# Order of two small loads on ScalarE's queue: bias ahead of w_phi

## The chip, the cores and the metric

The kernel runs on one core of one Trainium2 chip. The metric is the device time of one execution in microseconds; the time of a kernel is the median over its runs.

## The reference

The kernel computes one transformer block with two parallel branches on a layer-normed input: linear attention with a learned softmax feature map (w_phi) and an MLP with the Mish activation and a bias b1. S is 2048 tokens, D is 512, there are 32 heads of 16, and F is 1792. All inputs and the output are bf16.

```python
xn = layernorm(x)                                   # (1, 2048, 512)
q, k, v = split(xn @ wqkv)                          # 32 heads of 16 each
pq, pk = q @ w_phi, k @ w_phi                       # per head, 16 x 16
phi_q = concat(softmax(pq), softmax(-pq))           # 32 features
phi_k = concat(softmax(pk), softmax(-pk))
kv, z = phi_k^T v, sum_s(phi_k)
A = (phi_q kv / (phi_q z + 1e-6)) @ wo
h = xn @ w1 + b1
B = (h * tanh(softplus(h))) @ w2
out = x + A + B
```

## The kernel before

The tokens are worked in 16 tiles of 128 and in four groups of four tiles. Layer norm runs per tile: statistics on VectorE (L164, L166), the root on GpSimd (L170, L171), centring on VectorE (L175). The normed tile is transposed into `xnT`, for the first four tiles with TensorE (`ptr`, L562, copied by L581), later by transposing DMAs (L180). w_phi is not applied to keys and queries as such: it is folded into the key and query weights. For that, `Wbd` (L526, VectorE) spreads the loaded w_phi (`wsrc`) into a block-diagonal matrix, the key weights are transposed (`wT`: one half by TensorE, `ptw` L569, copied by ScalarE at L575; the other half by a transposing DMA, L482), and `pfold` (L150) multiplies the two; L159 writes the folded weights back into `wkp`. The first logits (`pl`, L203) use them; `pv` (L188) projects the values with `wv`. `ph` (L222) is the hidden layer, 56 units of four products, and L233 applies Mish with the bias `b1f`.

The bias comes in as a tile of 14 rows of 128 (`b1b`), is transposed by TensorE (`pb`, L535), and VectorE copies it to `b1f` (L622).

The order of the work on each engine is written out by hand: the string `STEPS` lists the steps, and each engine takes its instructions in that order. The first steps matter here:

```python
TW 0 @0; TW 1 @1; LS 0; LS 1; RS 0; PB @2; KM; AZ 0; TK 0 a; RS 1; DX 2; WB; TP 0 @3; F0 0 @4; AZ 1;
TP 1 @5; TK 1 a; FD 0 a; TC 0 v; F0 1 @0; F0 2 @1; FD 1 a; F0 3 @3; FD 2 a; TC 1 v; LS 2; RS 2; FD 3
```

TW is `ptw`, LS, RS and AZ are statistics, root and centring of one tile, PB is the bias transpose, TK the copy into `wT`, WB is `Wbd`, TP and TC the transposes and their copies, F0 and FD fold and write back, KM a small mask, DX a load of tokens, LP the first logits.

The loads of the prologue stand ahead of these steps, in program order, and each goes to the queue of the engine that issues it. SP's queue has token tiles 0 and 1 (L477), half of the key weights into `wkp` (L481), the transposing load (L482), token tiles 2 and 3 (L488), `wv` (L489), the first half of w1 (L490), the next four token tiles (L491), the second half of w1 (L492), and then L598. ScalarE's queue has two loads and a table load (L494). DMA completion semaphores are reused in turn, so an issue from L490 on waits for an earlier load to be complete. TensorE starts with twelve products of constants (`warm`, L512) ahead of its first step.

Of the kernel before, what the change touches and what calls it, by code (L numbers as in the profile page):

```python
# [62 lines left out]
def kernel(  # L63
# [12 lines left out]
    nc = tc.nc  # L76
# [17 lines left out]
    b1_v = B_b1.rearrange("(f p) -> f p", p=P)  # L94
# [21 lines left out]
    b1b = wts.tile([FT, P], BF16, name="b1b")  # L116
# [359 lines left out]
    for t in range(2):  # L476
# [5 lines left out]
    nc.sync.dma_start_transpose(  # L482
        out=wT_of[0][:, :, 2 * P : 4 * P], in_=A_wqkv[2 * P : 4 * P, D : 2 * D]
    )
    with nc.allow_non_contiguous_dma(reason="tiny w_phi load"):
        nc.scalar.dma_start(wsrc[:], wphi_v)
    nc.scalar.dma_start(b1b[:], b1_v[:, :])
    nc.sync.dma_start(x_sb[:, 2:4, :], x_v[:, 2:4, :])  # L488
    nc.sync.dma_start(wv[:], wqkv_v[:, :, 2 * D : 3 * D])  # L489
    nc.sync.dma_start(w1_sb[:, :, 0 : 7 * P], w1_v[:, :, 0 : 7 * P])  # L490
# [183 lines left out]
```

## Time and profile before

| what | value |
|---|---|
| time, median of 3 runs | 174.84 us (174.81 to 175.28) |
| profiled execution, its own time | 173.67 us |
| span of the profiled execution | 171.9 us |
| TensorE busy | 168.4 us, 98% of the span |
| VectorE busy | 145.1 us, 84% |
| ScalarE busy | 118.5 us, 69% |
| w_phi, from issue to landing | 2.4 us |
| granted TensorE clock | 1.00 |

The span runs from the first to the last instruction of one profiled execution; the time of that execution is 1.8 us longer. In the profile PE is TensorE's products, PEld its weight loads, DVE VectorE, ACT ScalarE, POOL GpSimd, SP SyncE; a "q" behind an engine's name is its sequencer, which issues the DMAs. Starts and lengths are in microseconds from the start of the span. The products are pipelined, so the rows of neighbouring ones overlap; the chain of waits lays them end to end.

### The profile page before, as it was taken

Reading aid. Unit: us, or ns where it says so; the run is one execution under the profiler, and the core shown is the slowest. Engines: PE = TensorE matmul, PEld = TensorE weight load, DVE = VectorE, ACT = ScalarE, POOL = GpSimd, SP = SyncE. Lnnn points to the kernel's source line nnn. Section 1 sums busy time; section 2 is a strip of 40 time slices with the busy share of each in tenths; the row PEclk is TensorE's granted clock in tenths of the full one; section 3 lists DMA queues with packets and bytes.
Section 4 is the critical chain, followed back from the end, with each engine's and each line's share of the span. In section 5 each row is a group of like instructions: output and inputs, shape, how many; then the busy total and the mean of one; then the engine's idle time right before and its main releaser. Section 6 shows DMA issues by size and latency. Waiting matters only on the chain.

```text
span 171.9 us, 2727 instructions
## 1 busy us (share of the span) xinstructions
PE 168.4 (98%) x1047; PEld 83.1 (48%) x1047; DVE 145.1 (84%) x224; ACT 118.5 (69%) x191; POOL 9.5 (6%) x26
## 2 busy tenths in 40 slices
PE   8999999999999999999999999999999999999993
PEld 2744444444454454454444744454545444554452
DVE  2878998999689999989999899898899987884333
ACT  2637899997998999899878968966722546632200
POOL 4332103200000000000000000000000000000000
PEclk9999999999999999999999999999999999999999
DMA  5997180689910000000000444036583737769831
GB/s 139 289 373 244 31 215 0 122 135 262 345 57 0 0 4 0 0 0 4 0 0 0 75 90 83 0 59 130 93 159 114 137 83 150 141 141 215 141 101 61
DMA packets 44185, 18.02 MB, mean 105 GB/s; under 512 B 35980, under 2 KB 44172, under 8 KB 44172
## 3 DMA queue, kind: packets, MB, share of 16 engines
q1 hardware_dynamic: 43472, 17.73, 44.1%
q10 hardware_dynamic: 700, 0.12, 0.4%
q8 instruction: 8, 0.13, 0.3%
q14 instruction: 5, 0.04, 0.1%
HBM read 7.10 MB, written 2.10 MB: 53 GB/s over the span
## 4 chain that ended last, share of the span: by engine, by line
PE 98%; DVE 0%; issue 0%
PE po L456 28%; PE ph L222 28%; PE pl L188 14%; PE pv L188 8%; PE po L463 8%; PE warm L512 3%; PE pnd L411 2%; PE pkv L380 2%; PE pfold L150 1%; PE pl L203 1%; PE pwide L188 1%; PE ptr L562 1%; PE ptw L569 0%; DVE x_sb L470 0%; PE pb L535 0%
## 5 line engine op out<-in xcount | busy, mean ns | idle before, releaser
L456 PE MATMUL po<-w_sb,acts 128*128 128x512 bf16 (+2 forms) x238 | 51.0, 366 | 0.0
L222 PE MATMUL ph<-xnT,w_sb 128*128 128x512 bf16 x224 | 49.8, 379 | 0.0
L233 ACT ACTIVATE acts<-ph,b1f 128x512 bf16<-128x512 f32 x56 | 36.3, 698 | 5.4 <-PE ph L222 5.3
L299 DVE TENSOR_REDUCE s<-e 128x128 f32<-128x2048 bf16 x16 | 36.0, 2278 | 1.7 <-ACT e L282 1.7
L222 PEld LDWEIGHTS <-w_sb 128*128 128x128 bf16 x224 | 21.7, 98 | 25.7
L456 PEld LDWEIGHTS <-acts 128*128 128x128 bf16 x238 | 22.2, 98 | 24.2
L282 ACT ACTIVATE e<-e 128x2048 bf16<-128x2048 bf16 x16 | 30.2, 1911 | 0.1
L188 PEld LDWEIGHTS <-xnT 128*128 128x128 bf16 x184 | 17.5, 98 | 20.3 <-DMA wv<-in_A_wqkv_dram 0.5
L470 DVE TENSOR_TENSOR x_sb<-po,x_sb 128x512 bf16<-128x512 f32 (+2 forms) x17 | 11.1, 656 | 8.6 <-PE po L463 8.6
L426 ACT COPY ds<-pnd 128x32 f32<-128x32 f32 x16 | 3.0, 186 | 22.0 <-PE pnd L411 22.0
L188 PE MATMUL pv<-wv,xnT 128*128 128x512 bf16 x64 | 15.8, 379 | 0.0
L246 ACT CAST p_sb<-pl 128x512 bf16<-128x512 f32 x23 | 12.9, 592 | 4.0 <-PE pl L188 4.0
L463 PE MATMUL po<-wqk,xnT 128*128 128x512 bf16 (+2 forms) x68 | 15.4, 366 | 0.0
L188 PE MATMUL pl<-wqk,xnT 128*128 128x512 bf16 x64 | 15.1, 379 | 0.0
L164 DVE BATCH_NORM_STATS2 stats<-x_sb 128x6 f32<-128x512 bf16 x16 | 10.1, 679 | 4.2 <-DMA x_sb<-in_A_x_dram 4.2
L257 DVE TENSOR_TENSOR m<-m 128x512 bf16<-128x512 bf16 (+1 forms) x32 | 11.5, 359 | 1.1
L188 PE MATMUL pl<-wkp,xnT 128*128 128x512 bf16 x48 | 11.8, 379 | 0.0
L257 DVE TENSOR_TENSOR m<-p_sb 128x1024 bf16<-128x1024 bf16 x16 | 10.9, 683 | 0.1
L266 DVE TENSOR_TENSOR e<-p_sb,m 128x2048 bf16<-128x2048 bf16 x8 | 9.8, 1225 | 0.8 <-PE pkv L380 0.5
L266 DVE TENSOR_TENSOR e<-m,p_sb 128x2048 bf16<-128x2048 bf16 x8 | 9.8, 1225 | 0.3
L333 DVE TENSOR_TENSOR e<-e,r 128x2048 bf16<-128x2048 bf16 x8 | 9.4, 1220 | 0.4 <-ACT r L308 0.4
L138 ACT ACT_TABLE_LOAD x7 | 9.0, 1283 | 0.1
(66 smaller groups left out, 134.5 us busy)
## 6 DMA issues: line engine op xcount, KB each, us to landing
w_sb<-in_B_w_dram SPq DMA_DIRECT2D x4, 896.0 KB, 7.1
out_dram<-x_sb SPq DMA_DIRECT2D x15, 128.0 KB, 1.9
x_sb<-in_A_x_dram SPq DMA_DIRECT2D x3, 512.0 KB, 8.0
wv<-in_A_wqkv_dram SPq DMA_DIRECT2D x1, 512.0 KB, 5.1
wqk<-in_A_wo_dram SPq DMA_DIRECT2D x1, 512.0 KB, 4.2
x_sb<-in_A_x_dram SPq DMA_DIRECT2D x2, 128.0 KB, 2.3
wkp<-in_A_wqkv_dram SPq DMA_DIRECT2D x1, 256.0 KB, 3.0
x_sb<-in_A_x_dram SPq DMA_DIRECT2D x1, 256.0 KB, 3.4
```

What stands on the lines that cost most here:

```text
L164: nc.vector.bn_stats(stats[:, i, :], xs[:, i, :])
L188: nc.tensor.matmul(pp, lhsT=xnT[:, t, kt, :], rhs=w[:, kt, :], start=(kt == 0), stop=(kt == KT - 1),)
L222: nc.tensor.matmul(ph_of[u][:], lhsT=w1_sb[:, kt, f * P : (f + 1) * P], rhs=xnT[:, g * TPG : (g + 1) * TPG, kt, :], start=(kt == 0), stop= ...
L233: nc.scalar.activation(acts[:, f, g * 512 : (g + 1) * 512], ph_of.pop(u)[:], ACT.Mish, bias=b1f[:, f : f + 1])
L246: copy(p_of[s][:, i, :], pl_of.pop((s, i)))
L257: nc.vector.tensor_tensor(out=m[:], in0=src[:, :, 0:half], in1=src[:, :, half : 2 * half], op=op)
L266: nc.vector.tensor_tensor(out=e_of[s][:].rearrange("p t j l c -> p (t j) l c")[:, :, pl, :].rearrange("p t (c e o) -> p t c e o", e=8, o=2 ...
L282: nc.scalar.activation(v, v, ACT.Exp)
L299: nc.vector.reduce_sum(t[:], pair(s, k).rearrange("p t j l (c e) -> p (t j l c) e", e=16), axis=AX.X)
L456: nc.tensor.matmul(po_of[t, c.stop][:, c], lhsT=acts[:, f, t * P : (t + 1) * P], rhs=w2_sb[:, f, c], start=(f == 0), stop=False,)
L463: nc.tensor.matmul(po_of[t, c.stop][:, c], lhsT=oT_of[t // 2][:, t % 2 * 4 + j, :], rhs=wo_sb[:, j, c], start=False, stop=(j == 3),)
L470: nc.vector.tensor_tensor(out=y, in0=po_of.pop((t, c.stop))[:, c], in1=y, op=ALU.add)
```

## The change

The issue of the bias load is moved ahead of the issue of the w_phi load. Both stay on ScalarE's queue, and both stay ahead of the table load.

```diff
@@ -482,9 +482,9 @@
     nc.sync.dma_start_transpose(
         out=wT_of[0][:, :, 2 * P : 4 * P], in_=A_wqkv[2 * P : 4 * P, D : 2 * D]
     )
+    nc.scalar.dma_start(b1b[:], b1_v[:, :])
     with nc.allow_non_contiguous_dma(reason="tiny w_phi load"):
         nc.scalar.dma_start(wsrc[:], wphi_v)
-    nc.scalar.dma_start(b1b[:], b1_v[:, :])
     nc.sync.dma_start(x_sb[:, 2:4, :], x_v[:, 2:4, :])
     nc.sync.dma_start(wv[:], wqkv_v[:, :, 2 * D : 3 * D])
     nc.sync.dma_start(w1_sb[:, :, 0 : 7 * P], w1_v[:, :, 0 : 7 * P])
```

The bias load is 14 rows of 256 bytes (3.5 KB); the w_phi load is 128 partitions of four pieces of 32 bytes (16 KB). The bias load is L487 before and L485 after; the w_phi load is L486 before and L487 after.

## The prediction

> **What bounds the kernel now.** I read the page first, for the engine that is full:
>
> ```profile
> PE 168.4 (98%) x1047; PEld 83.1 (48%) x1047; DVE 145.1 (84%) x224; ACT 118.5 (69%) x191; POOL 9.5 (6%) x26
> ```
>
> TensorE is busy 98% of the span, and the page's chain of waits is TensorE from end to end. A change can move the time only if it moves the point from which TensorE runs without a gap, or opens a gap later. So I read the chain in order of time over the first 10 us (columns: start us, length us, what):
>
> ```profile
> 0.82 4.32 PE warm L512 x12
> 5.14 0.78 PE ptw L569 x8
> 5.92 0.11 PE pb L535
> 6.03 0.33 PE ptr L562 x4
> 6.36 0.29 PE pfold L150 x4
> 6.64 0.22 PE ptr L562 x4
> 6.87 0.71 PE pfold L150 x12
> 7.58 1.79 PE pl L203 x8
> 9.37 1.01 PE pv L188 x4
> ```
>
> Before 5.14 there are only the warm-up products of L512, a fixed list that waits for no data. Then come eight products that transpose half of the key weights (ptw, L569), the bias transpose (pb, L535), two token transposes (ptr) and sixteen weight folds (pfold), the first logits (pl, L203), and from 9.37 the value projection (pv). One such projection of four products takes 0.86 us later in the same view; the first takes 1.01. So 0.15 us is lost there, and the waits of the weight loads say to what (columns: us in total, times, longest):
>
> ```profile
> PEld L188 <- DMA wv<-in_A_wqkv_dram: 0.5, 1, 0.5
> ```
>
> The weight loads sat 0.5 us before wv landed, most of it in the shadow of the logits still running. After that only one more weight load waits at all (0.2 us for a tile of tokens, in the shadow of a projection), and the waits of the products themselves list none to the end of the kernel.
>
> Third, the timeline of the first microseconds, for the two loads that change places and for those who read them (start us, length us, engine, line):
>
> ```profile
> 0.78 0.46 ACTq L486 DMA_DIRECT2D wsrc<-in_A_w_phi_dram  x1
> ...
> 0.79 0.87 SPq L477 DMA_DIRECT2D x_sb<-in_A_x_dram  x2
> ...
> 1.27 0.74 ACTq L487 DMA_DIRECT2D b1b<-in_B_b_dram  x1
> ...
> 1.71 0.43 SPq L481 DMA_DIRECT2D wkp<-in_A_wqkv_dram  x1
> ...
> 2.18 1.32 SPq L482 DMA_TRANSPOSE wT<-in_A_wqkv_dram  x1
> ...
> 5.32 0.42 DVE L526 TENSOR_TENSOR Wbd<-block,wsrc 128x512 bf16<-128x512 bf16 x1
> ...
> 5.85 0.18 PE L535 MATMUL pb<-ident,b1b 14*128 14x14 bf16 x1
> 5.88 0.41 DVE L175 TENSOR_SCALAR xn<-x_sb,mv,rstd 128x512 bf16<-128x512 bf16 x1
> ```
>
> The two loads leave ScalarE's queue at 0.78 and 1.27. Their readers run at 5.32 (Wbd on VectorE, from wsrc) and 5.85 (pb on TensorE, from b1b). The DMA issues give the time from issue to landing in the last column:
>
> ```profile
> wkp<-in_A_wqkv_dram SPq DMA_DIRECT2D x1, 256.0 KB, 3.0
> ...
> wsrc<-in_A_w_phi_dram ACTq DMA_DIRECT2D x1, 16.0 KB, 2.4
> b1b<-in_B_b_dram ACTq DMA_DIRECT2D x1, 3.5 KB
> ```
>
> So w_phi lands at 0.78 + 2.4 = 3.2 us, and wkp, which starts the real TensorE work, at 1.71 + 3.0 = 4.7. For the bias the view has no time; the trace's semaphore records have its last update at 3.7 us.
>
> **The change part by part.** Nothing is added or removed. In the built programs all engines have the same instructions in the same order, but for the two issues on ScalarE's queue. No issue of SP or GpSimd is passed.
>
> *The bias moves up.* It issues at 0.78 instead of 1.27 and lands about 0.5 us sooner than 3.7. Its reader pb stood in TensorE's order behind ptw, which ends at 5.92, and started as ptw ended: it had 2.1 us of cover and gets more. Gain 0. The next reader, b1f on VectorE at 9.46, and the first Mish at 14.79 are further still.
>
> *w_phi moves down.* It now issues when the bias's issue ends. That row is 0.74 us where it stood second; the other row is 0.46. As the first issue it may take either, so w_phi issues between 1.27 and 1.53, later by 0.5 to 0.75, and with the same 2.4 us it lands at 3.7 to 4.0. The reader Wbd starts at 5.32, right behind the centring of token tile 0 on VectorE (from 4.99, 0.41 us long). Cover 1.3 us, cost 0. Beyond this cover: queued behind Wbd on VectorE is the centring of tile 1 (5.88), which waits for its own GpSimd root until 5.84, and whose transpose runs on TensorE at 6.48; it ends at 6.29, so it has 0.2 us to spare, and Wbd's own reader pfold starts at 6.25, 0.5 us after Wbd ends at 5.74. Wbd could therefore start some 0.3 us late, at 5.6, for nothing; every microsecond after that is one on the chain.
>
> *ScalarE behind both issues.* The table load at 2.05 follows both in either order, and both rows together are the same 1.2 us. ScalarE's first data instruction is at 5.61, after 2.27 us of waiting for TensorE. Cost 0.
>
> *Completion slots.* The built program reuses DMA completion semaphores: SP's load of the first w1 half (L490, issued at 4.67) waits for the slot of the ScalarE queue's first load, the second half (L492, 5.78) for that of its second. They now wait for the bias (about 3.2) and for w_phi (4.0 at the latest). Both are done first. Cost 0, up to a landing of w_phi at 5.78.
>
> *Company on the DMA engines.* This is the only part with a price. w_phi is 512 pieces of 32 bytes; the trace's packets have them at 2.17 to 2.79 us, among the pieces of the first token tiles. Moved by 0.5 to 0.75 us they run at 2.7 to 3.5, beside the first pieces of wkp (3.0 to 4.2). While w_phi ran, the token pieces came at 32 to 48 in 0.2 us, against 62 to 72 without it: it takes about 0.4 of the engines for 0.62 us, 0.25 us of work. From 3.0 to 3.4 only 43 pieces moved where some 130 fit, so most of w_phi falls into a hole. wkp is later by between 0 and 0.62 us (all of w_phi ahead of it); I take 0.15. It landed at 4.75. TensorE can use it from 5.14; with a weight load of 0.15 and the 0.08 between landing and load it must be there by 4.91. Cover 0.16 us, so my value costs 0, and the bound costs 0.62 - 0.16 = 0.46. If wv, three issues later on the same queue, slips too, the 0.15 us that TensorE already waits for it covers nothing; if it stays, that takes 0.15 off. From below: the token tiles lose w_phi's company and land up to 0.25 us sooner, but tile 0 feeds VectorE work that is followed by TensorE's fixed order, and the most that an earlier stream of loads returns is the 0.15 us of waiting for wv. So this part lies between -0.15 and +0.46; I take +0.05, near the end where the hole absorbs it.
>
> The Trainium skill (Perfetto Trace Analysis, DMA Instruction — HWDGE) says that the descriptor generator is shared by the issuing queues and locked by one DMA at a time, so that an issue can include a wait for the lock. By that, w_phi's 0.46 us could stand in front of wkp's issue at 1.71, and the sum would be 0.46 - 0.16 = 0.3 us. The trace does not bear this out as a full lock: ScalarE's issue at 0.78 and SP's two at 0.79 ran side by side, and SP's rows did not stretch.
>
> **The sum.** 0 + 0 + 0 + 0 + 0.05 us. The profiled execution took 173.67 us (span 171.9 and 1.8 around it); that becomes 173.72. The median of the three runs, 174.84, is 1.17 us above the profiled execution, so the forecast is 174.84 + 0.05, say 174.9. This kernel's three runs lie 0.27% apart, so 0.3%, or 0.52 us, is about the least that a measurement can tell from no change.
>
> **The rivals.**
>
> *w_phi lands behind the transposed weights (slower).* If its many small pieces, now second on their queue, are prepared only after SP's issues of 1.71 and 2.18, they follow the transposing load, whose last semaphore is at 5.96, and need their 0.62 us: landing 6.6. Wbd starts at 6.6 instead of 5.32, 1.0 us after the 5.6 from which it decides; less 0.15 for wv, the chain is 0.85 us longer: 175.7. For it: SP's transposing issue is the longest there, 1.32 us. Against it: the bias, second on the same queue, issued at 1.27 and had its packets at 2.82, ahead of wkp's at 3.0. Chance 0.10.
>
> *wkp takes the whole collision and nothing covers it (slower).* wkp is later by 0.62 us, the loads behind it as well, and TensorE starts 0.46 late; with the small stalls that a shifted hand-written order can open later, each like the 0.15 for wv, it passes 0.52: about 175.4. For it: wkp's cover is only 0.16 us. Against it: the hole at 3.0 to 3.4. Chance 0.07.
>
> *The first loads speed up (faster).* The token tiles come sooner, the stream moves up, and TensorE gains the wv wait (0.15) and the small gaps in pl (1.79 for 8 products that take 1.73), ptr (0.33 against 0.22) and pfold (0.29 against the 0.24 of its later ones): 0.37 us at most, 174.5. That is under 0.52, because the warm-up list holds TensorE until 5.14 whatever lands earlier; it needs some scatter of the runs on top. Chance of being read as faster: 0.09.
>
> *Nothing reaches the loads at all*: if w_phi still lands ahead of its readers, the time is the forecast's, whatever the packets do.
>
> **How the numbers follow.** Forecast, within 0.3%: 0.74. Slower by over 0.3%: 0.10 + 0.07 = 0.17. Faster by over 0.3%: 0.09. The range: below, 174.84 - 0.15 and a scatter of about 0.3 us, 174.4; above, 174.84 + 0.46 and the 0.44 by which the highest run exceeds the median, 175.7, which also takes in the first rival.
>
> **What would show it.** In the profile after, L485 should be the first issue of ScalarE's queue at 0.78 and w_phi (L487) follow at 1.27 to 1.53; Wbd still at about 5.3, pb at about 5.85; ptw at 4.9 to 5.0 behind the same warm-ups; pv's first row at 9.3 to 9.4 with the wait for wv ahead of it. A wait of VectorE's Wbd for w_phi's DMA would show the first rival; a wait of ptw's weight load for wkp the second. The forecast is wrong if pv's first product starts over 0.5 us from 9.37, or if TensorE shows a wait after 10 us.

## The result, and the profile after

| | before | after |
|---|---|---|
| time, median of 6 runs each | 174.98 us (174.63 to 175.28) | 173.93 us (173.35 to 174.13) |
| ratio, 95% interval | | 0.9934 (0.9908 to 0.9959) |
| profiled execution, its own time | 173.67 us | 173.99 us |
| its span | 171.9 us | 172.3 us |

The change is 0.66% faster, 1.05 us; the forecast of 174.9 us, no change, and its range from 174.4 are missed on the fast side. One thing stands out before any trace is opened: the profiled execution of before took 173.67 us, below every one of its six timed runs and slightly less than the profiled execution of after. So the two profiles at hand show no gain, and cannot. The trace of before on which the prediction was built is one of a rarer kind of execution.

The chain of waits of after, first 10 us (start us, length us, what):

```profile
5.14 0.84 PE ptw L569 x8
5.99 0.11 PE pb L535
6.10 0.33 PE ptr L562 x4
...
7.06 0.42 DVE xnT L581
7.48 0.61 DVE stats L164
...
8.30 0.59 DVE wkp L159
...
8.93 0.59 PE pl L203 x2
9.52 0.86 PE pv L188 x4
```

The warm-ups still end at 5.14, ptw and pb follow as before, and the value projection pv starts at 9.52 instead of 9.37. Between them the chain now leaves TensorE for VectorE: copy of tile 1, statistics of tile 2, fold copy of wkp, and back to the last two logits. The timeline has the moved loads and their readers:

```profile
0.79 0.66 ACTq L485 DMA_DIRECT2D b1b<-in_B_b_dram  x1
...
1.48 0.41 ACTq L487 DMA_DIRECT2D wsrc<-in_A_w_phi_dram  x1
...
1.70 0.43 SPq L481 DMA_DIRECT2D wkp<-in_A_wqkv_dram  x1
...
5.27 0.42 DVE L526 TENSOR_TENSOR Wbd<-block,wsrc 128x512 bf16<-128x512 bf16 x1
...
5.92 0.09 PEld L535 LDWEIGHTS <-b1b 14*128 14x128 bf16 x1
```

The bias leaves at 0.79 and w_phi at 1.48, both as forecast, and Wbd starts at 5.27, about as forecast; pb starts at 5.92, right behind ptw. The DMA issues, last column from issue to landing:

```profile
wkp<-in_A_wqkv_dram SPq DMA_DIRECT2D x1, 256.0 KB, 3.4
x_sb<-in_A_x_dram SPq DMA_DIRECT2D x1, 256.0 KB, 3.4
...
wsrc<-in_A_w_phi_dram ACTq DMA_DIRECT2D x1, 16.0 KB, 3.8
```

w_phi takes 3.8 us instead of 2.4: 1.48 + 3.8 = 5.3, just as Wbd starts. wkp takes 3.4 instead of 3.0, and the weight loads of ptw now wait for it:

```profile
PEld L569 <- DMA wkp<-in_A_wqkv_dram: 0.2, 1, 0.2
```

By all of this the changed kernel should be a little slower. The gain had to be in what the one profile of before did not show.

### The profile page after: what moved, and what is told of

Its sections match the earlier page's. It is cut to its first block, busy times and chain, and to the rows that moved or that the text cites. A ratio compares the mean times of both kernels' runs of the same rounds, so it can differ in the third digit from the quotient of the medians.

```text
span 172.3 us, 2711 instructions
## 1 busy us (share of the span) xinstructions
PE 167.7 (97%) x1031; PEld 82.9 (48%) x1047; DVE 145.1 (84%) x224; ACT 118.4 (69%) x191; POOL 9.5 (5%) x26
## 4 chain that ended last, share of the span: by engine, by line
PE 91%; DVE 3%; DMA 3%; issue 1%; SPq 1%; DVEq 0%
PE ph L222 28%; PE po L456 24%; PE pl L188 14%; PE pv L188 7%; PE po L463 7%; DMA xnT<-wv 3%; PE warm L512 3%; PE pkv L380 2%; PE pnd L411 2%; PE pwide L188 1%; SPq L471 1%; PE pfold L150 1%; PE ptr L562 1%; DVE x_sb L470 1%; PE ptw L569 0%
## 5 line engine op out<-in xcount | busy, mean ns | idle before, releaser
L456 PE MATMUL po<-w_sb,acts 128*128 128x512 bf16 (+2 forms) x231 | 50.3, 366 | 0.3
```

The costliest lines, as they stand in the source:

```text
L456: nc.tensor.matmul(po_of[t, c.stop][:, c], lhsT=acts[:, f, t * P : (t + 1) * P], rhs=w2_sb[:, f, c], start=(f == 0), stop=False,)
```

## The experiments

**Before measured and traced twice more, after once more.** No edit.

> The kernel before, unchanged, for its spread and for another trace. The median of before was 174.98 us over six runs, and its one profiled execution 173.67, below all six. Theory A (in its usual execution a load of the prologue lands late and TensorE stalls early, the profiled execution having been a lucky one): runs at 174.6 to 175.3, and if the trace is of a usual run, TensorE's first value projection starts at 10.3 to 10.6 us instead of 9.37. Theory B (the difference is not in the early loads but in waits late in the kernel, such as the transposed attention output at 158 to 163 us): the first value projection at 9.3 to 9.6, and a wait of 0.5 to 1.5 us after 150 us. Theory C (drift between measurements, no difference): runs at 173.4 to 174.2, as those of the kernel after.

> The kernel before once more, for a third trace of it. Theory A: where the time is near 175, the first value projection starts about 1 us later than 9.37; where it is near 173.7, at about 9.37. Theory B: the value projection at 9.3 to 9.6 at either time, and the difference after 150 us.

> The kernel after, unchanged. Theories A and B: a median of 173.7 to 174.1 us, ratio to before 0.991 to 0.996. Theory C: ratio 0.998 to 1.002. In its trace the first value projection at 9.3 to 9.6 us, w_phi landing at about 5.2, just ahead of Wbd.

The kernel before again took 174.80 us in the median (12 runs, ratio to the other runs of before 0.9992, 0.9965 to 1.002); the kernel after 173.73 (12 runs, ratio 0.9942, 0.9919 to 0.9965). The gain is there again, so theory C, drift, is out. The new trace of before, of an execution of 174.74 us, has this chain:

```profile
3.55 4.87 DMA x_sb<-in_A_x_dram
...
8.44 0.71 DVE stats L164
...
9.17 0.18 DVE mv L166
9.35 0.59 DVE wkp L159
...
9.98 0.59 PE pl L203 x2
10.57 0.86 PE pv L188 x4
```

The load of token tiles 2 and 3 (issued at 3.55) lands 4.87 us later, at 8.42. VectorE's statistics of tile 2 wait for it, the fold copy of wkp stands behind them on VectorE's list, and the last two logits wait for that copy. pv starts at 10.57 instead of 9.37. The waits (total us, times, longest) and the DMA issues say the same:

```profile
PE pl L203 <- DVE wkp L159: 1.1, 1, 1.1
...
PEld L569 <- DMA wkp<-in_A_wqkv_dram: 0.5, 1, 0.5
```

```profile
x_sb<-in_A_x_dram SPq DMA_DIRECT2D x1, 256.0 KB, 4.9
```

In the first profile this load had 3.4. It has 16 completion records in the trace, as have the loads behind it; I call the part that one of them reports a share. These records tell more: fourteen lie between 6.98 and 7.06 us, the other two come at 8.13 and 8.42. One or two of the sixteen shares of the load are 1.1 to 1.4 us behind, and the same number of shares stays behind in the loads after it (value weights: fourteen by 8.53, then 9.62 and 9.89). In before_look2 (175.21 us) one share is behind: fifteen by 6.97, one at 8.92, pv at 11.07. The trace of after_again happened to be of its one execution near 175, 174.81 us: one share at 8.52 after fifteen by 6.90, pv at 10.68; the other eleven runs lie between 173.51 and 174.04. So theory A holds, and the kernels differ in how often it happens: over the runs of before that the kernels were compared with, 17 of 116 are below 174.2 us (from 0 of 6 to 10 of 31 in a single comparison), and of after 17 of 18.

The Trainium skill (DMA: Bandwidth & Descriptors, Queues, rings and completion order) says that a load is split over up to 16 engines and that each takes its parts from its own ring in order. The Trainium skill (DMA: Bandwidth & Descriptors, Why a DMA increments its semaphore by 16 and not by 1) says that the load has landed only when all of them have reported. The records above agree: the shares that are late in one load are as many as in the next, two and two in before_again, one and one in before_look2.

**Is the bias, landing late, what holds up TensorE?** pb_late: order of before, bias transpose moved behind the first logits.

```diff
-TW 0 @0; TW 1 @1; LS 0; LS 1; RS 0; PB @2; KM; AZ 0; TK 0 a; RS 1; DX 2; WB; TP 0 @3; F0 0 @4; AZ 1;
+TW 0 @0; TW 1 @1; LS 0; LS 1; RS 0; KM; AZ 0; TK 0 a; RS 1; DX 2; WB; TP 0 @3; F0 0 @4; AZ 1;
...
-v; LS 3; CB; LP i @4,5; V 1 @0; AZ 2; LC 0 0 v; RS 3; AZ 3; TP 2 @1; V 0 @3; LC 0 1 v; TC 2 a; TP 3
+v; LS 3; LP i @4,5; PB @2; CB; V 1 @0; AZ 2; LC 0 0 v; RS 3; AZ 3; TP 2 @1; V 0 @3; LC 0 1 v; TC 2 a; TP 3
```

> The kernel before with its order of loads, but the bias transpose pb and the copy to b1f are put behind the first logits on TensorE's list (about 9.3 us instead of 5.85), so a bias that lands late holds up nothing early. Theory A1 (in the usual execution of before the bias lands after 6 us and pb holds up TensorE's queue): as fast as the kernel after, ratio to before 0.991 to 0.996. Theory A2 (another load, wkp, a token tile or wv, is late because w_phi runs first): no change, ratio 0.998 to 1.002. Theory B: no change either.

174.81 us, ratio 0.9983 (0.996 to 1.0007): no change. A late bias is not what held TensorE up; another load is late (A2). In the trace of pb_late, too, one share of the token load is behind, landing at 8.38 after fifteen by 6.85.

**Fewer pieces of w_phi.** wphi_small leaves out w_phi of 24 of the 32 heads and uses that of the first eight for all:

```diff
-    wsrc = wts.tile([P, 4, DH], BF16, name="wsrc")
+    wsrc = wts.tile([P, 1, DH], BF16, name="wsrc")
...
-        nc.scalar.dma_start(wsrc[:], wphi_v)
+        nc.scalar.dma_start(wsrc[:], wphi_v[:, 0:1, :])
```

> The order of before (w_phi, then the bias), but w_phi is loaded for its first eight heads alone, 128 pieces of 32 bytes instead of 512, and Wbd uses these for all 32 heads. What is seen so far: in usual executions of before, one of the 16 shares of the load of token tiles 2 and 3 lands 1.4 to 2.0 us behind the other 15 (8.4 to 8.9 us instead of 7.0), VectorE's statistics of tile 2 wait for it, and the last fold copy of wkp queued behind them holds up the first logits. Theory P (the 512 pieces of w_phi at the head of ScalarE's queue leave one DMA engine behind): the token load lands at 7.0 to 7.3, time 173.5 to 174.0, ratio 0.992 to 0.996. Theory Q (the place of the bias, second on its queue, does it): lands at 8.4 to 8.9, ratio 0.998 to 1.002.

173.50 us, all ten runs between 173.31 and 173.65, ratio 0.9951 (0.9923 to 0.9979; in that comparison 10 of 31 runs of before were themselves near 173.6). The order is that of before; only 384 pieces of 32 bytes are gone, and the scatter with them. Its chain and its loads:

```profile
6.93 0.42 DVE xnT L581
7.36 0.61 DVE stats L164
...
8.17 0.59 DVE wkp L159
...
8.80 0.59 PE pl L203 x2
9.39 0.86 PE pv L188 x4
```

```profile
x_sb<-in_A_x_dram SPq DMA_DIRECT2D x1, 256.0 KB, 3.4
...
wsrc<-in_A_w_phi_dram ACTq DMA_DIRECT2D x1, 4.0 KB, 2.3
```

The statistics no longer wait, the sixteen shares of the token load land between 6.43 and 6.93, those of the value weights by 8.42. Theory P is borne out, Q is not.

**Moving one load past the table load.** Two kernels, both with pb behind the logits as in pb_late. In bias_late the table load stands between the two loads:

```diff
         nc.scalar.dma_start(wsrc[:], wphi_v)
+    nc.scalar.preload_act_table_set("mish")
     nc.scalar.dma_start(b1b[:], b1_v[:, :])
...
-    nc.scalar.preload_act_table_set("mish")
```

In wphi_late it stands ahead of both:

```diff
+    nc.scalar.preload_act_table_set("mish")
     with nc.allow_non_contiguous_dma(reason="tiny w_phi load"):
         nc.scalar.dma_start(wsrc[:], wphi_v)
     nc.scalar.dma_start(b1b[:], b1_v[:, :])
...
-    nc.scalar.preload_act_table_set("mish")
```

> w_phi first on ScalarE's queue as in before, then the table load, then the bias; the bias transpose stands behind the first logits, as in pb_late, so that it is not missed. Theory P (w_phi's early place): nothing changes, the token load lands at 8.4 to 8.9, ratio 0.998 to 1.002. Theory Q (the bias issued at 1.27, right behind w_phi and beside the issue of wkp): the token load lands at 7.0 to 7.3, ratio 0.992 to 0.996.

> The table load first on ScalarE's queue, then w_phi at about 2.1 us instead of 0.78, then the bias; the bias transpose behind the first logits as in pb_late. Theory P: the token load lands at 7.0 to 7.3 as in the kernel after; the time is 173.5 to 174.0 unless w_phi now lands after 5.6 us, beyond which Wbd holds up TensorE by as much. Theory Q (the bias second, right behind w_phi, does it): the token load still lands at 8.4 to 8.9 and the time is 174.8 or more.

These did not do what they were made for. The table load held up no issue behind it, as the timeline of wphi_late shows:

```profile
0.78 1.28 ACT L485 ACT_TABLE_LOAD   x1 [0.78 <-PEq L658]
...
0.81 0.46 ACTq L487 DMA_DIRECT2D wsrc<-in_A_w_phi_dram  x1
```

w_phi left at 0.81 instead of 2.1, and in bias_late the bias left at 1.31 instead of 1.27. bias_late took 174.66 us (ratio 1.002, 0.9993 to 1.0047) and is pb_late once more; in its trace five shares of the token load come late, the last at 8.19 after eleven by 7.26. wphi_late took 173.80 us, but its ratio is 0.9987 (0.9952 to 1.0022), with seven of ten runs below 174.2 and three at 174.6 to 175.0. It issues w_phi 0.02 us after token tile 0 instead of 0.01 us before it; whether that is what helped stays open. In its trace the 512 pieces run from 2.29 to 2.80 us, the same time as in the traces of before (2.17 to 2.79 in the first, 2.31 to 2.92 in before_again). So if this kernel is faster, later pieces are not the reason.

**Taking the fold copy out from behind the statistics.** fd3_first:

```diff
-TP 1 @5; TK 1 a; FD 0 a; TC 0 v; F0 1 @0; F0 2 @1; FD 1 a; F0 3 @3; FD 2 a; TC 1 v; LS 2; RS 2; FD 3
-v; LS 3; CB; LP i @4,5; V 1 @0; AZ 2; LC 0 0 v; RS 3; AZ 3; TP 2 @1; V 0 @3; LC 0 1 v; TC 2 a; TP 3
+TP 1 @5; TK 1 a; FD 0 a; TC 0 v; F0 1 @0; F0 2 @1; FD 1 a; F0 3 @3; FD 2 a; TC 1 v; FD 3
+v; LS 2; RS 2; LS 3; CB; LP i @4,5; V 1 @0; AZ 2; LC 0 0 v; RS 3; AZ 3; TP 2 @1; V 0 @3; LC 0 1 v; TC 2 a; TP 3
```

> The order of loads of before, but on VectorE's list the last fold copy of wkp (FD 3) is put ahead of the statistics of tile 2 (LS 2). Path theory (the late token load costs time because the fold copy is queued behind the statistics that wait for it): the first logits end at about 9.4 us also where the token load lands at 8.4 to 8.9; TensorE then waits for the value weights, whose last share is late as well (9.9 to 10.4 against 8.6), so the first value projection starts at 10.0 to 10.4 instead of 10.6 to 11.1: 0.4 to 0.7 us gained, ratio 0.996 to 0.998. Rival (the token load being late and the lost time have a common cause on another path): ratio 0.999 to 1.001.

174.70 us, ratio 1.001 (0.998 to 1.004): nothing gained, where the path theory had 0.4 to 0.7 us. In its trace, of the slowest of its ten executions (175.29), the logits no longer wait for the copy, and TensorE runs into the next late share instead:

```profile
4.16 6.79 DMA wv<-in_A_wqkv_dram
...
10.99 1.04 PE pv L188 x4
```

The value weights landed at 10.95 (a share 1.8 us behind) and pv started at 10.99. I had put 9.9 to 10.4 there. In this execution the queue on VectorE is only the first place where the wait is seen; behind it stands a late share in the next load. The other nine executions (174.34 to 175.00) have no trace, so that the same took their gain is not shown.

**The bias off the queue, w_phi in its early place.** bias_pool, with pb behind the logits:

```diff
-    nc.scalar.dma_start(b1b[:], b1_v[:, :])
+    nc.gpsimd.dma_start(b1b[:], b1_v[:, :])
```

> w_phi at 0.78 us on ScalarE's queue as in before; the bias is taken off that queue and issued by GpSimd, its transpose behind the first logits. Theory P1 (w_phi's early pieces): the token load still lands at 8.2 to 8.9, ratio 0.998 to 1.002. Theory P2 (the bias behind w_phi on ScalarE's queue): lands at 6.9 to 7.3, ratio 0.992 to 0.996.

174.99 us, ratio 1.0029 (1.0002 to 1.0056), none of ten runs below 174.7: no gain, if anything a little longer. Three shares of the token load are late (8.18 to 8.28), as the chain shows:

```profile
3.55 4.73 DMA x_sb<-in_A_x_dram
...
8.30 0.70 DVE stats L164
...
9.21 0.59 DVE wkp L159
...
10.55 0.97 PE pv L188 x4
```

P2 is out: with w_phi in its early place, taking the bias off the queue gains nothing.

**w_phi later, nothing ahead of it.** wphi_gated holds w_phi's issue back with a memset of its tile, with pb behind the logits:

```diff
+    make_identity(nc, ident[:])
+    nc.gpsimd.memset(wsrc[:], 0.0)
     with nc.allow_non_contiguous_dma(reason="tiny w_phi load"):
         nc.scalar.dma_start(wsrc[:], wphi_v)
     nc.scalar.dma_start(b1b[:], b1_v[:, :])
...
-    make_identity(nc, ident[:])
```

gated_pool is wphi_gated with the bias on GpSimd's queue, the same edit as in bias_pool.

> w_phi stays first on ScalarE's queue and the bias stays behind it, but w_phi's issue waits for a GpSimd memset of its tile, placed behind the identity, so that it leaves at about 1.5 us as in the kernel after, with nothing ahead of it on its queue; the bias leaves later still, and its transpose stands behind the first logits as in pb_late. Theory P1 (what counts is that w_phi's 512 pieces do not run beside token tile 0, wherever the bias is): the load of token tiles 2 and 3 lands at 6.9 to 7.3 us, ratio 0.992 to 0.996. Theory P2 (what counts is that the bias is out of the way early): lands at 8.4 to 8.9, ratio 0.998 to 1.002.

> As wphi_gated (w_phi leaves at about 1.5 us, alone on ScalarE's queue), but the bias is issued by GpSimd at about 1.5 us instead of following w_phi at 3.4. wphi_gated was near 173.7 us in six of ten executions and near 174.9 in four. Theory P1 (w_phi's pieces beside token tile 0 leave a share behind; the late bias of wphi_gated did the rest): the token load lands at 6.9 to 7.3, nine or ten of ten executions below 174.2, ratio 0.992 to 0.996. Theory P3 (having the bias's short load ahead on the same queue has a part of its own): again a mixture, ratio 0.996 to 0.999.

wphi_gated: 173.99 us, ratio 0.9968 (0.9938 to 0.9998), six runs at 173.6 to 174.05 and four at 174.7 to 175.0, a mixture; its bias left only at 3.43, as its issue waited for a completion slot. gated_pool: 174.07 us, ratio 0.9953 (0.9931 to 0.9974), all ten runs between 173.82 and 174.32. Its issues and Wbd:

```profile
1.49 0.73 POOL L489 DMA_DIRECT2D b1b<-in_B_b_dram  x1
1.50 0.45 ACTq L488 DMA_DIRECT2D wsrc<-in_A_w_phi_dram  x1
...
5.31 0.42 DVE L527 TENSOR_TENSOR Wbd<-block,wsrc 128x512 bf16<-128x512 bf16 x1
```

So moving w_phi's issue back, with no bias ahead of it on the queue, brings most of the gain, and none of these ten executions is near 175. Its token load landed at 7.55 in the trace, later than the 7.3 I had allowed, and eight of ten runs are below 174.2 where I had put nine or ten. Its ratio is a little above those of after (0.9934 and 0.9942), but the intervals overlap. The two kernels differ in the issue of the bias alone, and w_phi's pieces run at the same time in both (2.70 to 4.55 us in wphi_gated, 2.82 to 4.57 in gated_pool); why four executions of wphi_gated are near 175 all the same is not shown.

**More pieces.** wphi_twice loads w_phi twice in a row ahead of the bias.

```diff
+    wtwo = wts.tile([P, 4, DH], BF16, name="wtwo")
     with nc.allow_non_contiguous_dma(reason="tiny w_phi load"):
+        nc.scalar.dma_start(wtwo[:], wphi_v)
         nc.scalar.dma_start(wsrc[:], wphi_v)
```

> The order of before, but w_phi is loaded twice in a row, the first time into a tile that nothing reads: 1024 pieces instead of 512. Theory P: with 128 pieces the time was 173.5 us in every execution, with 512 usually 174.4 to 175.3; with 1024 the straggling share is later still, the token load lands at 9.0 to 10.5 and the time is 175.2 to 176.5, ratio 1.002 to 1.010. Rival (the number of pieces has no part in it, 128 pieces only being over before something else begins): as before, ratio 0.998 to 1.002.

175.08 us (174.66 to 175.47), ratio 1.0022 (1.0003 to 1.0041). All ten runs are near 175, the direction of theory P, but of before 27 of 31 were too in the same comparison, and the delay in the trace is no larger than usual: one share at 8.73, against 9.0 or more expected. From 128 to 512 pieces the runs follow theory P; from 512 to 1024 they show next to nothing more.

**w_phi through GpSimd.** wphi_pool is the kernel after with w_phi issued by `nc.gpsimd.dma_start`.

> The bias first on ScalarE's queue as in the kernel after, and w_phi issued by GpSimd on its own queue at about 0.8 us. Theory P1: its 512 pieces run in the same first microseconds, so if what counts is their company with token tile 0 the time is that of before, ratio 0.998 to 1.002; if they come only after 2.7 us, that of the kernel after, ratio 0.992 to 0.996, or worse by what Wbd waits beyond 5.6. Theory Q2 (the hardware queue of ScalarE has a part in it, whatever the time): ratio 0.992 to 0.996 with w_phi's pieces before 2.7 us.

173.77 us, ratio 0.9965 (0.9942 to 0.9987), ten runs from 173.62 to 174.32. Its 16 KB show in the trace as 16 packets of 1024 bytes from 3.88 to 4.28 us, not as 512 of 32. It lands at 5.06, in time for Wbd at 5.27. As the pieces did not come before 2.7 us, P1's first case and Q2 were not put to the test. Its ratio is just above the 0.996 that P1's second case allowed; the kernel is no better than after.

**Where does a share fall behind?** x23_first: order of before, the token load put ahead of the transposing load.

```diff
+    nc.sync.dma_start(x_sb[:, 2:4, :], x_v[:, 2:4, :])
     nc.sync.dma_start_transpose(
         out=wT_of[0][:, :, 2 * P : 4 * P], in_=A_wqkv[2 * P : 4 * P, D : 2 * D]
     )
...
-    nc.sync.dma_start(x_sb[:, 2:4, :], x_v[:, 2:4, :])
```

> The order of before on ScalarE's queue; on SP's queue the load of token tiles 2 and 3 is put ahead of the transposing load of wT. It is meant to be read in the trace. The transposed half lands later by some 0.7 us, so the folds of kt 2 and 3 wait and the time may be 0.3 to 1.0 us longer. Theory S1 (one engine falls behind during the transposing load): the 16 shares of the token load, now ahead of it, land within 0.5 us of each other, and the value weights behind it still show a last share 1 us or more late. Theory S2 (it falls behind earlier, at w_phi or wkp): the token load's last share is again 1 us or more behind the others.

174.57 us, ratio 0.9974 (0.994 to 1.0007), not the 0.3 to 1.0 us longer that I had expected. In its trace wkp itself, the load right after w_phi, has one share 0.8 us behind (5.36 and then 6.17), and TensorE waits for it:

```profile
PE ptw L569 <- DMA wkp<-in_A_wqkv_dram: 1.2, 1, 1.2
```

Neither theory is borne out. The value weights behind the transposing load land together, 9.34 to 9.41, where S1 had a late share; of the token load three shares land by 5.47 and thirteen together, 6.76 to 6.88, where S2 had one far behind the others. The late share of wkp does not settle it either: the pieces of the transposing load ran from 4.89 us on, before that share landed. It is one trace, and in the two new traces of before no share of wkp is late (the last thirteen land from 5.10 to 5.30, the last fifteen from 4.96 to 5.19). Where exactly a share falls behind, and why only one or a few of sixteen, stays open.

**The traces side by side.** The time of an execution follows from when pv starts (ten of the sixteen traces; the difference is that time less the start of pv, and the other six have 164.16 to 164.30):

| run | token load landed, us | pv starts, us | time of that execution, us | difference |
|---|---|---|---|---|
| wphi_small | 6.93 | 9.39 | 173.51 | 164.12 |
| before | 6.99 | 9.37 | 173.67 | 164.30 |
| after | 6.98 | 9.52 | 173.99 | 164.47 |
| wphi_pool | 7.28 | 9.44 | 173.66 | 164.22 |
| gated_pool | 7.55 | 9.81 | 174.17 | 164.36 |
| bias_pool | 8.28 | 10.55 | 174.91 | 164.36 |
| before_again | 8.42 | 10.57 | 174.74 | 164.17 |
| after_again | 8.52 | 10.68 | 174.81 | 164.13 |
| wphi_twice | 8.73 | 10.88 | 175.13 | 164.25 |
| before_look2 | 8.92 | 11.07 | 175.21 | 164.14 |

The difference varies by 0.35 us, the start of pv by 1.7. So what sets these executions apart is over by about 11 us. From the row of 7.28 on, pv starts 2.15 to 2.27 us after the token load has landed: a late share is passed on in full.

## Why the prediction was wrong

**What bounds the kernel** was right: TensorE runs without a gap once pv starts, and only the start of pv moves the time. So was the remark that a load of w_phi up to 5.6 us costs nothing: it landed at 5.24 and Wbd was on time.

**The terms at zero** held: the bias gained nothing for pb, ScalarE behind both issues was not touched, and the completion slots were clear in time.

**"Company on the DMA engines" failed, and with it the sum.** I had the right place, w_phi's 512 pieces at 2.17 to 2.79 us, and priced the wrong thing. I worked out what w_phi takes from the engines on average, 0.25 us, and put it on wkp. The runs show that with the 512 pieces in this place one or a few of the sixteen shares of the loads behind them come some 1 to 2 us late in most executions of before, and a load is as late as its last share. From below I set -0.15 us, "the most that an earlier stream of loads returns"; the measured change is -1.05. The cap was taken from a trace in which the token load had landed at 6.99 and held up nobody; in a usual execution the same load costs 1.2 us (pv at 10.57 against 9.37).

**The term for wkp is not borne out.** Against the first trace its sign is right and its size is not: wkp landed at 4.75 there and at 5.07 after, 0.32 us later where I took 0.15, and TensorE waited 0.2 us for it. But in the other two traces of before it landed at 5.30 and 5.19, with waits of 0.5 and 0.4 us, and in after_again at 5.12. So its landing differs more between executions than between the kernels, and these traces show no delay by the change. The time of w_phi was off as well: I gave it its old 2.4 us and a landing at 4.0; beside wkp it took 3.8.

**The 1.17 us were the clue.** I noted that the profiled execution was 1.17 us faster than the median of the runs, and added the change to the median as if the same trace stood behind it. Three runs from 174.81 to 175.28 and a profile at 173.67 do not come from one distribution of 0.27%; the gap is what the change mostly removes. My own sign of being wrong, pv more than 0.5 us from 9.37, could not catch it, as it was set by the same trace: pv of after started at 9.52. The two slower rivals did not come about: w_phi did not land behind the transposed weights (5.24 against 6.10 for them), and wkp was at most 0.3 us later. The faster rival had the right sign, but was held to 0.37 us by the same trace.

**What each theory is worth now.** Shown: the time of an execution goes with the start of pv, and that with the last share of the token load (the table). With a quarter of w_phi's pieces no execution is near 175 (wphi_small). With w_phi in its early place, neither reading the bias later (pb_late) nor taking its load off the queue (bias_pool) gains anything; moving w_phi back as well does (gated_pool). Not shown: why the later place of w_phi helps. That its pieces then no longer meet token tile 0 on the engines is an argument, and two kernels do not fit it. wphi_late has the pieces where before has them, and seven of its ten executions are below 174.2, against 10 of 31 of before beside it; wphi_gated has them where after has them (2.70 to 4.55 and 2.74 to 4.62 us), and four of its ten are near 175.

## What to carry to other kernels

Compare the time of the profiled execution with the runs before reading anything off it; where it lies outside them, the trace shows another case than the one that is measured, and a second profile is worth more than a closer look at the first. A load of many tiny pieces is not priced by its bytes: look at the last of the sixteen completions of the loads behind it, not at the mean rate. Try such a load in fewer pieces, or away from the first loads that somebody waits for; here the first helped in every run, the second in most. A stall on an engine's queue can have the next one right behind it, as in the trace of fd3_first: move the cause, not the first one who waits.

## What the runs showed of the hardware that I had not expected

- With 512 pieces of 32 bytes at the head of the second queue, one or a few of the sixteen shares of the loads behind them came some 1 to 2 us late in each of two new traces of before, and 99 of its 116 runs took 174.2 us or more. With 128 such pieces all ten runs were below 173.7.
- A table load on ScalarE (0.78 to 2.06 us in wphi_late) did not hold up the DMA issues that follow it in the same program: they left at 0.81 and 1.29.
- The same w_phi load issued by GpSimd (wphi_pool) appeared as 16 packets of 1024 bytes instead of 512 of 32.
